# Another order table for the first two thirds of an attention and mixture-of-experts kernel

## The chip, the cores and the metric

The kernel runs on one core of one Trainium2 chip. The metric is the device time of one execution in microseconds (us). The kernel before took 322.93 us, the median of three runs (321.3 to 323.65).

## The reference, cut to what matters

Three computations follow one another, all in float32.

1. **Linear attention** (2 batches, 8 heads, 576 tokens, head size 64, 128 features): `phi(x) = exp(h - max h)` with `h = x·omegaᵀ` less a row constant; then `kv = Σ k_p vᵀ`, `z = Σ k_p`, and `out = (q_p·kv) / (q_p·z + 1e-6)`.
2. **A gated product**: `a = x@w1`, `b = x@w2`, `h = (a*b)@w3`, `out = h@w_out`, with 1152 tokens, 512 model columns and 1024 inner columns. The two last products have nothing between them, so the kernel forms `W = w3@w_out` once.
3. **Mixture of experts**: `logits = x@w_gate`, `argmax` over 8 experts, softmax weight of the winner; every token goes to its expert (`w1`, relu, `w2`) as far as capacity lasts and is scaled by its weight.

The weights of part 2 come as 64-bit words; the kernel turns them into float32 on the chip.

## The kernel before, in words

A table, `ORDER` (line 36), is a list of words. Each word is one step (`t_` and the letters), its arguments, and behind `@` the bank of the matmul results that it takes. A loop runs the words from first to last, and what each step issues then stands in that order on its engine: on TensorE (PE), VectorE (DVE), ScalarE (ACT), GpSimd (POOL) and the DMA queue of SyncE (SP). Each of them works its own list strictly in order. A second string, `END`, orders what comes behind the table: the rest of part 2, the routing and the experts; it stays.

The steps that the prediction speaks of, with their lines:

- `LD`, `LDV`, `LDOM`, `LDCAP` (L241, L246, L231, L491): loads by SP: one of nine blocks of 128 tokens of k or q (256 KB), of v (260 KB), omega, and the capacity, which is spread to 96 partitions. `ZD` and `ZG` store zeros.
- `PJ.k1` (L253): the projection of a block on PE into a pair of banks. `MX` (L258): its row maxima on DVE. Then either `E0` and `E1` (L274): eight exponentials on ACT straight out of the banks, or `SUB` (L266) on DVE, which frees the banks, and `EX` (L269) on ACT. The next `PJ` of a pair waits until its banks are free.
- `KO` (L227) opens a pair of banks for the sums over tokens, `KV` (L299) adds a block of k to them, `KVZ` (L306) reads them out.
- `TR` (L310) transposes q on PE, `NUM` (L325) forms the numerators, `RD`, `X`, `XT`, `XH`, `XL` divide, transpose and split x in a high and a low part.
- A weight tile goes through `LDW` (L374, 512 KB, two raw buffers), `WA`, `WB`, `WC` (L381, L384, L387: three bit operations on DVE), `CAST` (L392, ACT, the high part) and `LOW` (L396, POOL, the low part, in one subtraction). The next but one `LDW` waits for this tile's `WC`. There are 40 tiles, `w10` to `w27`, `wo0` to `wo7` and `w300` to `w371`.
- `AB` (L403) is twelve matmuls of a tile with x; `ASB` and `G` (L408, L413) read and multiply; `TT` (L533) and `ST` (L538) turn the product and store it in DRAM. `W` (L427) forms the combined weight, `WR`, `WH`, `WL` read it out. `GT`, `GU`, `UC`, `LG` carry the gate through it.

Of the kernel before, what the change touches and what calls it, by code (L numbers as in the profile page):

```python
# [40 lines left out]
PJ.q2@2 EX.k8 WB.w12 KO.1@0 KV.6 MX.q2 EX.q1 KV.4b WC.w12 E0.q2 KV.7 MX.q4 LDW.w10 LD.q8 KV.5 E1.q2 WB.w20 KV.8 WC.w20 CAST.w12 MX.q3 LDW.w11 TR.2.0@2
KVZ.1 LOW.w12 TR.0.0@3 QT.2.0 TR.0.1@0 SUB.q3 TR.2.1@1 QT.0.0 TR.1.1@2 QT.0.1 WA.w10 TR.1.0@3 QT.2.1 WB.w10 NUM.0@6 QT.1.0 WC.w10 NUM.2@0 QT.1.1 RD.0
LDW.w13 E0.q4 X.0 NUM.1@2 RD.2 X.2 XT.0@6 CAST.w20 RD.1 XT.2@7 XH.0 LOW.w20 X.1 TR.4.0@0 XH.2 XL.0 XT.1@1 PJ.q6@2 XL.2 XH.1 CAST.w10 XL.1 PJ.q5@6
E1.q4 LOW.w10 MX.q6 AB.2.0.0@1 WA.w11 EX.q3 WB.w11 AB.0.0.0@4 E1.q6 WC.w11 MX.q5 LDW.w21 AB.0.0.1@5 CAST.w11 SUB.q5 QT.4.0 LOW.w11 ASB.0.0 TR.4.1@0
ASB.2.0 G.0.0 TR.3.0@4 WA.w13 TR.3.1@1 QT.3.0 AB.1.0.0@5 WA.w21 QT.3.1 WB.w13 QT.4.1 WB.w21 E0.q6 NUM.3@6 WC.w21 NUM.4@0 WC.w13 LDW.w22 CAST.w21 RD.3
LDW.wo0 PJ.q8@2 ASB.1.0 LOW.w21 RD.4 EX.q5 X.3 PJ.q7@4 X.4 CAST.w13 MX.q8 XT.3@6 LOW.w13 XT.4@7 XH.3 AB.1.0.1@0 XH.4 XL.3 E0.q8 XL.4 AB.3.0.0@1 MX.q7
E1.q8 AB.0.1.0@6 WA.w22 WB.w22 WC.w22 TR.5.1@7 ASB.0.1 AB.0.1.1@2 WA.wo0 LDW.w23 CAST.w22 WB.wo0 SUB.q7 LOW.w22 AB.1.1.0@3 WC.wo0 TR.6.1@6 G.0.1
CAST.wo0 LDW.w14 AB.2.1.0@4 TT.0.0 ASB.1.1 LOW.wo0 G.1.0 AB.2.0.1@5 WA.w23 WB.w23 WC.w23 AB.2.1.1@0 WA.w14 LDW.w300 WB.w14 AB.1.1.1@2 WC.w14 G.2.0
CAST.w14 LDW.wo2 AB.3.1.0@3 CAST.w23 G.1.1 TT.1.0 ASB.2.1 LOW.w23 EX.q7 TR.6.0@2 G.2.1 TR.5.0@5 LOW.w14 QT.6.0 TT.2.0 TR.7.0@4 QT.5.0 TR.8.0@0
AB.3.0.1@2 QT.5.1 WA.wo2 QT.6.1 WA.w300 WB.w300 ASB.3.0 NUM.6@6 QT.8.0 WB.wo2 NUM.5@0 QT.7.0 WC.wo2 ASB.3.1 WC.w300 LDW.wo3 CAST.wo2 AB.3.1.1@3 RD.6  # L50
LDW.w24 CAST.w300 RD.5 X.6 LOW.w300 TR.7.1@5 X.5 XT.6@4 QT.7.1 TR.8.1@6 G.3.0 LOW.wo2 AB.4.1.0@7 G.3.1 QT.8.1 TT.3.0 XH.6 XT.5@5 WA.wo3 ST.0.0.1
NUM.7@0 XL.6 ST.0.0.3 XH.5 XL.5 NUM.8@2 WB.wo3 AB.3.2.0@6 WA.w24 WB.w24 WC.wo3 AB.0.2.0@4 WC.w24 CAST.wo3 LDW.w320 ASB.3.2 RD.8 LOW.wo3 LDW.wo1
AB.1.2.0@5 CAST.w24 X.8 ST.0.0.2 RD.7 X.7 LOW.w24 AB.2.2.0@6 WA.w320 AB.0.2.1@2 WB.w320 ASB.2.2 WC.w320 XT.8@3 WA.wo1 CAST.w320 LDW.wo6 XT.7@6
ST.0.0.0 WB.wo1 XH.8 AB.3.2.1@0 XH.7 LOW.w320 XL.8 ASB.1.2 XL.7 AB.2.2.1@1 WC.wo1 CAST.wo1 LDW.w310 WA.wo6 AB.0.3.0@3 G.3.2 LOW.wo1 ASB.0.2 G.0.2
WB.wo6 AB.1.3.0@6 WC.wo6 WA.w310 CAST.wo6 LDW.wo4 AB.0.3.1@0 WB.w310 ASB.0.3 WC.w310 AB.2.3.0@5 G.0.3 CAST.w310 LOW.wo6 LDW.wo7 TT.0.1 ASB.1.3
AB.4.3.0@4 LOW.w310 CONSTV LGM@0 WA.wo4 AB.1.2.1@6 WB.wo4 WA.wo7 AB.1.3.1@2 WC.wo4 WB.wo7 CAST.wo4 LDW.wo5 AB.2.3.1@3 WC.wo7 G.1.3 LOW.wo4 LDW.w301
G.1.2 ASB.2.3 AB.3.3.0@2 G.2.2 CAST.wo7 TT.1.1 ASB.4.3 LOW.wo7 W.0.0@6 G.2.3 ASB.3.3 TT.2.1 ASB.4.1 WA.w301 WB.w301 AB.3.3.1@1 WA.wo5 WC.w301
AB.4.1.1@7 CAST.w301 LDW.w350 G.3.3 TT.3.1 LOW.w301 W.1.0@1 ST.0.1.0 WB.wo5 WC.wo5 WA.w350 CAST.wo5 LDW.w351 ST.0.1.3 WB.w350 AB.4.0.0@5 WC.w350
CAST.w350 LOW.wo5 LDW.w15 AB.4.3.1@4 ST.0.1.1 LOW.w350 W.0.1@-1 WA.w351 WB.w351 WC.w351 W.5.0@3 LDW.w321 CAST.w351 WA.w15 G.4.1 WH.0 LOW.w351 WR.0
WB.w15 W.2.0@2 WC.w15 CAST.w15 LDW.w360 WA.w321 WB.w321 WC.w321 AB.4.2.0@7 LOW.w15 LDW.w16 ST.0.1.2 AB.4.2.1@6 WA.w360 ASB.4.2 CAST.w321 WB.w360  # L60
WC.w360 W.5.1@-1 G.4.2 CAST.w360 LOW.w321 LDW.w370 WA.w16 WB.w16 AB.5.1.0@7 WH.5 WC.w16 CAST.w16 LOW.w360 LDW.w311 AB.5.0.0@6 ASB.5.1 ASB.4.0 WA.w370
G.4.3 LOW.w16 W.2.1@-1 WB.w370 WC.w370 AB.6.0.0@7 WA.w311 CAST.w370 LDW.w340 WB.w311 WR.2 WC.w311 AB.4.0.1@5 CAST.w311 LOW.w370 LDW.w330 WH.2 W.6.0@4
LOW.w311 G.4.0 WA.w340 WB.w340 W.1.1@-1 WC.w340 WA.w330 CAST.w340 LDW.w341 TT.4.1 LOW.w340 GT.0@2 WB.w330 WR.1 AB.6.1.0@5 ASB.6.0 WC.w330 WR.5 WA.w341
LDW.w331 WH.1 W.4.0@7 WB.w341 CAST.w330 WC.w341 TT.4.0 LOW.w330 LDW.w361 W.7.0@3 CAST.w341 WA.w331 LOW.w341 WA.w361 W.4.1@-1 WB.w331 WC.w331 WB.w361
CAST.w331 LDW.w371 WC.w361 W.3.0@1 CAST.w361 LOW.w331 LDW.w25 ASB.5.0 LOW.w361 W.3.1@-1 WA.w371 WB.w371 WC.w371 WA.w25 CAST.w371 LDW.w26 GT.1@6 WB.w25
WTC.0 W.6.1@-1 WTC.1 WC.w25 WH.3 LOW.w371 LDW.w17 CAST.w25 WR.3 LOW.w25 W.7.1@-1 WH.4 WA.w26 WB.w26 WC.w26 WG@2 AB.5.0.1@6 WGC WA.w17 LDW.w27 WR.6
WB.w17 CAST.w26 WC.w17 GU.0@1 GU.1@2 UC.0 LOW.w26 LG.0 UC.1 CAST.w17 LG.1 G.5.0 ASB.6.1 WL.2 AB.5.1.1@1 WR.4 WR.7 LOW.w17 AB.6.1.1@2 G.5.1 TT.5.0 WL.1
GT.2@5 G.6.1 GT.5@1 WA.w27 AB.7.1.0@6 WTC.5 WB.w27 WC.w27 AB.7.0.0@7 CAST.w27 LOW.w27 AB.6.0.1@2 ASB.7.0 WL.5 AB.7.0.1@1 G.6.0 WL.4 TT.6.0 GT.6@7 WH.6
# [1033 lines left out]
```

## Time and profile before

| What | Value |
|---|---|
| median of three runs | 322.93 us |
| the profiled execution's own time | 322.64 us |
| its span | 320.9 us |
| PE busy | 307.9 us (96%) |
| DVE / ACT / POOL busy | 209.3 / 130.4 / 107.4 us |
| granted TensorE clock, mean | 0.999 |

The span is the profiled stretch of the execution; 1.74 us of the execution's own time lie around it. An engine's busy time is the union of its instructions; what is left of the span it waited. A row of a timeline gives the start, the length, the engine, the line and operation, how many instructions are merged, and in brackets the idle time before and what ended it.

### The profile page before, as it was taken

The page shows a single profiled execution, that of the slowest core. Times are in us where ns is not written, and L with a number is a line of the kernel's source. Part 1 is how long each engine was busy: PE and PEld are TensorE (multiplying, and loading weights), DVE is VectorE, ACT ScalarE, POOL GpSimd, SP SyncE. Part 2 cuts the span into 40 slices and gives each one's busy share as a digit, 9 for nine tenths or more (in the row PEclk, how much of TensorE's full clock was granted, in tenths as well). Part 3 has the DMA queues.
Part 4 walks back from the last instruction along what each step waited for, and adds up shares of the span by engine and source line. Part 5 has one row for each costly group of instructions (what it writes and reads, how often), then busy time and mean ns, then how long its engine had stood idle before and what let it go on. Part 6 is the DMA issues. An engine that isn't in the chain of part 4 may idle for free. (4 is left out here: it accounts for less than half of the span.)

```text
span 320.9 us, 7411 instructions
## 1 busy us (share of the span) xinstructions
PE 307.9 (96%) x3045; PEld 286.9 (89%) x3045; DVE 209.3 (65%) x381; ACT 130.4 (41%) x301; POOL 107.4 (33%) x96
## 2 busy tenths in 40 slices
...
GB/s 180 401 314 385 193 68 77 122 137 127 176 183 185 133 132 163 211 171 160 167 131 151 178 2 2 141 11 251 161 237 150 203 231 66 93 133 49 1 27 53
DMA packets 25180, 47.77 MB, mean 149 GB/s; under 512 B 3148, under 2 KB 12492, under 8 KB 25142
## 3 DMA queue, kind: packets, MB, share of 16 engines
...
q10 hardware_dynamic: 2368, 1.18, 2.8%
...
q14 instruction: 13, 0.11, 0.1%
...
## 5 line engine op out<-in xcount | busy, mean ns | idle before, releaser
L403 PE MATMUL banks<-xh,w_hl 128*128 128x288 f32 x416 | 87.9, 298 | 1.1 <-DVE g L413 1.0
L396 POOL TENSOR_TENSOR w_hl<-w_f,w_hl 128x512 fp32r<-128x512 f32 x32 | 43.6, 1364 | 111.1 <-ACT w_hl L392 111.1
L403 PEld LDWEIGHTS banks<-xh,w_hl 128*128 128x128 f32 x416 | 67.9, 188 | 2.4 <-DVE g L413 1.2
L403 PE MATMUL banks<-xl,w_hl 128*128 128x288 f32 x208 | 61.4, 295 | 0.0
L427 PE MATMUL banks<-wo_hl,w_hl 128*128 128x512 f32 x192 | 46.0, 395 | 0.0
L427 PEld LDWEIGHTS banks<-wo_hl,w_hl 128*128 128x128 f32 x192 | 35.5, 188 | 7.9 <-POOL w_hl L396 0.2
L392 ACT CAST w_hl<-w_f 128x512 fp32r<-128x512 f32 x32 | 20.0, 627 | 49.5 <-DVE w_f L387 49.4
L403 PEld LDWEIGHTS banks<-xl,w_hl 128*128 128x128 f32 x208 | 39.1, 188 | 0.2
L387 DVE SCALAR_TENSOR_TENSOR w_f<-w_raw,w_f 128x512 uint32<-128x512 uint32 x32 | 28.8, 903 | 0.9
L381 DVE TENSOR_SCALAR w_f<-w_raw 128x512 uint32<-128x512 uint32 x32 | 17.8, 555 | 16.3 <-DMA w_raw<-in_w 13.7
L258 DVE TENSOR_REDUCE mx<-banks 128x8 f32<-128x1024 f32 x18 | 21.6, 1218 | 9.5 <-PE banks L253 9.1
L814 PE MATMUL banks<-r_xc,W 128*128 128x288 f32 x192 | 26.8, 297 | 0.0
L814 PEld LDWEIGHTS banks<-r_xc,W 128*128 128x128 f32 x192 | 25.8, 188 | 0.1
L384 DVE SCALAR_TENSOR_TENSOR w_f<-w_raw,w_f 128x512 uint32<-128x512 uint32 x32 | 24.6, 772 | 0.8
L533 DVE STREAM_TRANSPOSE gs<-g 128x576 f32<-128x576 f32 x16 | 19.8, 1238 | 4.4 <-POOL g L562 4.1
L553 PE MATMUL banks<-xh,w_hl 128*128 128x288 f32 x96 | 20.2, 299 | 0.0
L396 POOL TENSOR_TENSOR wo_hl<-wo_f,wo_hl 128x512 fp32r<-128x512 f32 x8 | 11.4, 1431 | 18.8 <-ACT wo_hl L392 18.8
L413 DVE TENSOR_TENSOR g<-a_sb,banks 128x288 f32<-128x288 f32 x26 | 11.5, 448 | 9.0 <-PE banks L403 5.6
L731 POOL TENSOR_TENSOR r_e_00l<-r_e_0r,r_e_00h 128x512 fp32r<-128x512 f32 x4 | 6.0, 1512 | 30.4 <-ACT r_e_00h L727 15.1
L553 PEld LDWEIGHTS banks<-xh,w_hl 128*128 128x128 f32 x96 | 15.7, 188 | 0.6 <-issue 0.5
L408 ACT COPY a_sb<-banks 128x288 f32<-128x288 f32 x26 | 10.2, 403 | 12.7 <-PE banks L403 9.4
L852 POOL DMA_INDIRECT out<-r_yo,r_odx x6 | 5.6, 938 | 25.6 <-DVE r_yo L849 16.4
...
## 6 DMA issues: line engine op xcount, KB each, us to landing
w_raw<-in_w SPq DMA_DIRECT2D x32, 512.0 KB, 4.5
wo_raw<-in_wo SPq DMA_DIRECT2D x8, 512.0 KB, 4.6
...
r_e_0r<-in_e SPq DMA_DIRECT2D x4, 512.0 KB, 4.1
```

The source lines that it names most:

```text
L258: V.tensor_reduce(out=mx, in_=heads(at["pj", n]), axis=AX, op=ALU.max, negate=True)
L381: V.tensor_scalar(out=f, in0=word(w, 1), scalar1=3, scalar2=0x3FFFFFF8, op0=ALU.logical_shift_left, op1=ALU.bitwise_and)
L384: V.scalar_tensor_tensor(out=words_of[w], in0=word(w, 1), scalar=0xC0000000, in1=words_of[w], op0=ALU.bitwise_and, op1=ALU.bitwise_or)
L387: V.scalar_tensor_tensor(out=words_of[w], in0=word(w, 0), scalar=29, in1=words_of[w], op0=ALU.logical_shift_right, op1=ALU.bitwise_or)
L392: A.copy(out=t[:, 0], in_=words_of[w].bitcast(F32))
L396: nc.gpsimd.tensor_tensor(out=h[1], in0=words_of[w].bitcast(F32), in1=h[0].bitcast(F32), op=ALU.subtract)
L403: nc.tensor.matmul(out=banks[:, b, :C], lhsT=hl[s][:, k, :], rhs=xhl[int(c)][r][:, k], start=(n == 0), stop=(n == 11))
L413: V.tensor_tensor(out=g_t[int(f)][:, int(c) * C:(int(c) + 1) * C], in0=abp.pop((f, c)), in1=banks[:, at["ab", f, c, "1"], :C], op=ALU.mult)
L427: nc.tensor.matmul(out=banks[:, at["W", f]], lhsT=w[s][:, k % 4, :], rhs=hl_of[f"wo{k}"][r], start=(k == 0 and (s, r) == (0, 0)), stop=(k ...
L533: V.transpose(out=sts[f // GF, b][:, :, :, f % GF], in_=g_t[f][:, b * S:(b + 1) * S].rearrange("p (j t) -> p j t", t=32))
L553: nc.tensor.matmul(out=p[:, :C], lhsT=hl[s][:, k, :], rhs=xhl[c][r][:, k], start=(n == 0), stop=(n == 11))
L814: nc.tensor.matmul(out=p4[d][:, :C], lhsT=w_t[f][:, s, d * 128:(d + 1) * 128], rhs=xc[r][f // 4][:, f % 4], start=(f == 0 and (s, r) == (0 ...
```

## The change

The 31 lines of `ORDER` are replaced by 31 others: the same kinds of steps on the same data in another order, many with other banks. The table was found by a search that scores a table as the mean over several draws of durations. Nothing else is changed: no step's code, not `END`, no buffer count. Two lines of the table, of 62 in the difference:

```diff
 ORDER = """
-LD.k1 CONST WU@0 LDOM LD.k3 LDCAP LD.k4 LDW.w20 LD.q0 LD.k2 OMS IDENT LD.k6 LD.k0 PJ.k1@2 LD.k5 ZM LDV.3 ZG.1 PJ.k4@4 MX.k1 PJ.k3@6 MX.k4 E0.k1 LDV.1
...
+LDOM CONST WU@0 LD.k1 LD.q0 LD.k4 LD.k0 LD.k6 LD.k3 OMS LDV.4 ZM LD.k2 IDENT LD.k5 PJ.k1@2 LDV.2 PJ.q0@4 MX.k1 LDV.1 PJ.k4@6 LD.k7 MX.q0 E0.k1 PJ.k0@0
...
```

**TensorE, the first projections.** `k1_97` is the block k1, `om_s` the scaled omega; each row is eight matmuls, one `PJ`. Before:

```order
L253 MATMUL banks_84<-om_s_87,k1_97 128x128 x8
L253 MATMUL banks_84<-om_s_87,k4_134 128x128 x8
L253 MATMUL banks_84<-om_s_87,k3_131 128x128 x8
L253 MATMUL banks_84<-om_s_87,q0_138 128x128 x8
L253 MATMUL banks_84<-om_s_87,k0_149 128x128 x8
L253 MATMUL banks_84<-om_s_87,k5_159 128x128 x8
L253 MATMUL banks_84<-om_s_87,k2_140 128x128 x8
```

Now:

```order
L253 MATMUL banks_84<-om_s_87,k1_129 128x128 x8
L253 MATMUL banks_84<-om_s_87,q0_131 128x128 x8
L253 MATMUL banks_84<-om_s_87,k4_133 128x128 x8
L253 MATMUL banks_84<-om_s_87,k0_135 128x128 x8
L253 MATMUL banks_84<-om_s_87,k3_139 128x128 x8
L253 MATMUL banks_84<-om_s_87,k5_152 128x128 x8
L253 MATMUL banks_84<-om_s_87,k2_146 128x128 x8
```

The first four projections take the four pairs of banks; q0 and k0 moved in front of k3, which is now the first that reuses a pair (k1's). On DVE the maxima of k1, q0, k4 and k0 now stand in a row, and `SUB.k4`, `MX.k3`, `SUB.k0`, `MX.k5`, `MX.k2`, `SUB.k2` follow; before it was the maxima of k1, k4, k3, then `SUB.k4`, the maxima of q0 and k0, and `SUB.k0`.

**The DMA queue of SP.** Its head before:

```order
L241 DMA k1_97<-in_kT 128x512
L231 DMA om_sb_129<-in_om 128x256
L241 DMA k3_131<-in_kT 128x512
L491 DMA cap_u_89<-in_cap 96x2
L241 DMA k4_134<-in_kT 128x512
L374 DMA w20_raw_136<-in_w2 128x1024
L241 DMA q0_138<-in_qT 128x512
```

Where the capacity's load stands now, with the stores of zeros (`out_0`) around it:

```order
L241 DMA q5_371<-in_qT 128x512
L241 DMA q6_425<-in_qT 128x512
L374 DMA w10_raw_545<-in_w1 128x1024
L477 DMA out_0<-zero_144 128x3x512
L491 DMA cap_u_89<-in_cap 96x2
L374 DMA w13_raw_591<-in_w1 128x1024
L374 DMA w11_raw_671<-in_w1 128x1024
```

The capacity went from fourth to 37th place, behind the load of w10; the first weight tile also left the head (it is now 19th), and one store of zeros stands between w10 and w13. Before, all stores of `out` stood in front of w10.

**VectorE, the weight tiles in the middle.** `w310_f` is the tile that `WA`, `WB` and `WC` make. Before:

```order
L381 TENSOR_SCALAR wo1_f_1450<-wo1_raw_1390 128x512
L384 SCALAR_TENSOR_TENSOR wo1_f_1450<-wo1_raw_1390,wo1_f_1450 128x512
L362 TENSOR_TENSOR xl3_1303<-banks_84,xh3_1302 128x4x128 x2
L387 SCALAR_TENSOR_TENSOR wo1_f_1450<-wo1_raw_1390,wo1_f_1450 128x512
L381 TENSOR_SCALAR wo6_f_1498<-wo6_raw_1454 128x512
L413 TENSOR_TENSOR g3_1283<-a_sb_1383,banks_84 128x288
L413 TENSOR_TENSOR g0_831<-a_sb_1514,banks_84 128x288
L384 SCALAR_TENSOR_TENSOR wo6_f_1498<-wo6_raw_1454,wo6_f_1498 128x512
L387 SCALAR_TENSOR_TENSOR wo6_f_1498<-wo6_raw_1454,wo6_f_1498 128x512
```

Now:

```order
L381 TENSOR_SCALAR wo1_f_1469<-wo1_raw_1407 128x512
L384 SCALAR_TENSOR_TENSOR wo1_f_1469<-wo1_raw_1407,wo1_f_1469 128x512
L387 SCALAR_TENSOR_TENSOR wo1_f_1469<-wo1_raw_1407,wo1_f_1469 128x512
L381 TENSOR_SCALAR w310_f_1489<-w310_raw_1446 128x512
L384 SCALAR_TENSOR_TENSOR w310_f_1489<-w310_raw_1446,w310_f_1489 128x512
L387 SCALAR_TENSOR_TENSOR w310_f_1489<-w310_raw_1446,w310_f_1489 128x512
L413 TENSOR_TENSOR g0_1042<-a_sb_1422,banks_84 128x288
L362 TENSOR_TENSOR xl3_1290<-banks_84,xh3_1289 128x4x128
L413 TENSOR_TENSOR g3_1268<-a_sb_1530,banks_84 128x288
L381 TENSOR_SCALAR wo6_f_1547<-wo6_raw_1491 128x512
L384 SCALAR_TENSOR_TENSOR wo6_f_1547<-wo6_raw_1491,wo6_f_1547 128x512
L387 SCALAR_TENSOR_TENSOR wo6_f_1547<-wo6_raw_1491,wo6_f_1547 128x512
```

The three operations of a tile now mostly stand together; other work went between tiles. Over the last 26 tiles (w320 on), eleven tiles had something between their `WA` and `WC` before, and five have it now.

## Rows read from the trace of the kernel before

**Rows 1.** The page: busy us of each engine (share of the span), instructions.
```profile
PE 307.9 (96%) x3045; PEld 286.9 (89%) x3045; DVE 209.3 (65%) x381; ACT 130.4 (41%) x301; POOL 107.4 (33%) x96
```

**Rows 2.** PE's waits: total us, times, longest.
```profile
PE banks L253 <- DMA k<-in_kT: 3.3, 3, 1.3
...
PE banks L403 <- DVE g L413: 1.0, 1, 1.0
```

**Rows 3.** PE by stretch: length, busy us (instructions), clock, DMA share, GB/s.
```profile
5.13:36.66 31.53, 26.06 (x550) 1.00 0.94 338
36.66:113.70 77.04, 76.93 (x846) 1.00 0.48 132
113.70:116.00 2.30, 1.33 (x10) 1.00 0.64 198
116.00:203.07 87.07, 86.83 (x771) 1.00 0.48 135
203.07:315.90 112.83, 112.73 (x861) 1.00 0.48 123
```

**Rows 4.** PE's timeline at the start.
```profile
5.13 1.51 PE L253 MATMUL banks<-om_s,k 64*128 64x128 f32 x16
7.71 2.06 PE L253 MATMUL banks<-om_s,k 64*128 64x128 f32 x32 [1.07 <-DMA k<-in_kT]
...
15.98 0.38 PE L227 MATMUL banks<-zeros 128*128 128x260 f16 x2 [1.22 <-DVE k0p L266]
16.29 1.15 PE L299 MATMUL banks<-v,k3p 128*64 128x65 f32 x32
...
36.66 0.66 PE L310 MATMUL banks<-ident,q2p 128*128 128x128 f32 x4
```

**Rows 5.** DVE's timeline at the start.
```profile
6.69 1.22 DVE L258 TENSOR_REDUCE mx<-banks 128x8 f32<-128x1024 f32 x1 [6.69 <-PE banks L253]
8.92 2.36 DVE L258 TENSOR_REDUCE mx<-banks 128x8 f32<-128x1024 f32 x2 [1.01 <-PE banks L253]
...
18.23 1.22 DVE L266 TENSOR_TENSOR k2p<-banks,mx 128x1024 f32<-128x1024 f32 x1
19.37 1.21 DVE L258 TENSOR_REDUCE mx<-banks 128x8 f32<-128x1024 f32 x1
```

**Rows 6.** ACT's timeline at the start.
```profile
7.95 2.17 ACT L274 ACTIVATE k1p<-banks,mx 128x128 f32<-128x128 f32 x8 [3.62 <-DVE mx L258]
...
19.11 1.11 ACT L269 ACTIVATE k0p<-k0p 128x1024 f32<-128x1024 f32 x1
```

**Rows 7.** DMA in 0 to 3.9 us, in 3.9 to 6.4, in 6.4 to 14.4.
```profile
DMA packets 359, 0.53 MB, mean 136 GB/s; under 512 B 37, under 2 KB 165, under 8 KB 359
...
DMA packets 270, 0.30 MB, mean 121 GB/s; under 512 B 126, under 2 KB 126, under 8 KB 270
...
DMA packets 1453, 3.17 MB, mean 397 GB/s; under 512 B 161, under 2 KB 161, under 8 KB 1453
```

**Rows 8.** DVE's waits, the longest line.
```profile
DVE w_f L381 <- DMA w_raw<-in_w: 13.7, 14, 3.1
```

**Rows 9.** Waits of PE's weight loads.
```profile
PEld banks L427 <- POOL w_hl L396: 0.2, 1, 0.2
```

**Rows 10.** DVE by line, 20 to 36 us: busy us, mean ns, idle before.
```profile
L387 DVE SCALAR_TENSOR_TENSOR w_f<-w_raw,w_f 128x512 uint32<-128x512 uint32 x2 | 1.4, 688 | 0.0
...
L381 DVE TENSOR_SCALAR w_f<-w_raw 128x512 uint32<-128x512 uint32 x2 | 0.8, 418 | 0.0
```

**Rows 11.** DVE by line, 100 to 190 us.
```profile
L387 DVE SCALAR_TENSOR_TENSOR w_f<-w_raw,w_f 128x512 uint32<-128x512 uint32 x20 | 20.6, 1031 | 0.7
L384 DVE SCALAR_TENSOR_TENSOR w_f<-w_raw,w_f 128x512 uint32<-128x512 uint32 x20 | 16.4, 820 | 0.5
L381 DVE TENSOR_SCALAR w_f<-w_raw 128x512 uint32<-128x512 uint32 x20 | 12.7, 633 | 13.1 <-DMA w_raw<-in_w 10.6 <-POOL w_hl L396 2.4
```

**Rows 12.** DMA issues: KB each, median us to landing.
```profile
w_raw<-in_w SPq DMA_DIRECT2D x32, 512.0 KB, 4.5
```

More of the change, by code (lines that the diff above doesn't have):

```diff
@@ L41 @@
[L41 to L68, printed above, removed]
@@ L69 @@
-WL.3 G.7.0 GT.3@2 WTC.2 AB.7.1.1@4 WTC.3 WTC.6 GU.3@1 GU.5@5 UC.3 GU.2@2 ASB.7.1 LG.3 UC.2 G.7.1 UC.5 GT.7@1 TT.7.0 GT.4@2 WTC.7 LG.2 WTC.4 ST.1.0.1
-GU.6@1 LG.5 ST.1.0.2 UC.6 ST.1.0.3 GU.4@2 GU.7@1 ST.1.0.0 UC.4 LG.6 UC.7 WH.7 LG.4 WL.7 WL.0 WL.6
+LDOM CONST WU@0 LD.k1 LD.q0 LD.k4 LD.k0 LD.k6 LD.k3 OMS LDV.4 ZM LD.k2 IDENT LD.k5 PJ.k1@2 LDV.2 PJ.q0@4 MX.k1 LDV.1 PJ.k4@6 LD.k7 MX.q0 E0.k1 PJ.k0@0
+LD.q8 LDV.0 MX.k4 E1.k1 LDV.3 MX.k0 LD.q1 E1.q0 LD.k8 PJ.k3@2 SUB.k4 LDW.w20 ZG.1 E0.q0 MX.k3 PJ.k5@6 LDWG LDV.5 SUB.k0 E1.k3 PJ.k2@4 LDV.6 LDW.w12
```

35 lines of the change are left out of this document (32 added, 3 removed).

## The prediction, on record before the changed kernel ran

> **What bounds the kernel now.** I read the page first: PE is busy for 96% of the span, every other engine for 65% or less [rows 1]. So I asked when PE is not busy, stretch by stretch [rows 3]. The reader should see how uneven it is. From 5.13 to 36.66 us, where PE runs the projections and the sums over k, it idles 31.53 - 26.06 = 5.47 us. From there to its last matmul it idles 0.11 + 0.97 + 0.24 + 0.10 = 1.42 us in 279 us, and 0.97 of that is one gap near 115 us, where an `AB` waited for the `G` that frees its bank [rows 2, 3]. The granted clock is 1.00 in every stretch, so nothing is to be had there. The change keeps all matmuls; it can win or lose only idle time of PE: some 6.9 us at most, 5.5 of it at the start.
>
> The start is paced by two things. One is the loads: three gaps, 3.3 us, end with a block of k landing [rows 2]. The other is DVE: it begins at 6.69 us, waits 1.01 us for the second projection, and PE then waits 1.22 us for `SUB.k0` [rows 4, 5]. The DMA rows tell why k4 was late: from 3.9 to 6.4 us the queue moved 121 GB/s with 126 packets under 512 B, behind that 397 GB/s [rows 7]. The capacity's load (96 rows of one word, fourth in the queue) stands there. At the later rate the 2.5 us would have moved 0.99 MB and not 0.30: a loss of 1.7 us for all loads behind it.
>
> **The start, step by step.** Durations are those of before: a projection 1.03 us (two in 2.06), the first one 1.51; a `KV` about 1.1 [rows 4]; `MX` and `SUB` 1.22 us long and 1.14 from start to start (18.23 to 19.37) [rows 5]; eight exponentials 2.17 us, an `EX` 1.1 [rows 6].
>
> PE starts k1 at 5.13 us as before (the warm-up matmuls set that), then q0, k4 and k0 without a pause, until about 9.75 us. Their loads and omega are 1.18 MB (four times 0.262 and 0.131). Even if the slow 2.5 us came all the same, 0.53 + 0.30 MB would have moved by 6.4 us, and k0 would be in 0.9 us later at 397 GB/s, at about 7.3 us, before PE wants it at 8.7 [rows 7]: the gain does not hang on my reading of the capacity.
>
> DVE, from 6.69 us in steps of 1.14: `MX` k1, q0 7.83, k4 8.97, k0 10.11, `SUB.k4` 11.25, `MX.k3` 12.39, `SUB.k0` 13.53, `MX.k5` 14.67, `MX.k2` 15.81, `SUB.k2` 16.95, and so on to `SUB.q1` 22.65 and `SUB.k8` 25.8, with the first steps of two weights (0.42 us each) in between [rows 5, 10].
>
> PE then waits three times. k3 takes k1's banks and waits for its exponentials, 7.95 + 2.17 = 10.1 us [rows 6]: 0.35 us. k5 waits for `SUB.k4`, 11.25 + 1.22 = 12.47, having been free at 11.2: 1.3 us. `KO.0` waits for `SUB.k0`, 14.75, having been free at 14.55: 0.2 us. After that PE has `KV`s between its projections and, step by step, comes at about the moment it may: k7 needs `SUB.k2` (18.2) and PE is there at 18.2; q2 needs `SUB.q1` (23.9) and PE is there at 24.5; `KO.1` needs `SUB.k8` (27.0) and PE is there at 27.6. That makes 1.85 us of idle time; with 0.15 for the tight ones, 2.0 against 5.47. **First term: -3.5 us**, and the first transposes come at about 33.2 us rather than 36.66 [rows 4]. Bounds: -3.6 (no other wait) and -2.5 (each of the three tight places 0.3 us late).
>
> The other engines come along. DVE's own list up to the same point (all maxima, `SUB.q3`, the first two weights) ends near 34.0 us, as against 37.6, so it is ahead by as much. The first `LDW` that waits for a raw buffer goes out behind `WC.w12` at about 29.3 us, not 32.6.
>
> **The rest of the table.** Here no sum can be made of removed work, since nothing is removed. Before, waits after 36.66 us come to 1.42 us. The gap of 0.97 has its cause in one place of the old order (a `G` that stood in DVE's list behind the operations of two tiles, wo4 and wo7), and that sequence is gone; but an order unknown to the trace will have small waits of its own. Their bounds are 0 and, from a weight path that does not follow (first rival), about 3 us; nearest are the 1.42 us that the old order had here. I take 0.8. **Second term: 0.8 - 1.42 = -0.6 us.**
>
> Edits that I cost at nothing: other banks (what waits is in the walk above); the stores of zeros and the capacity moved behind w10 (the capacity is first used in the middle of the table; the cover of these transfers is the time until w11 is due, third rival); the stores of the products, twelve as before; the `END` part, whose instructions are the same and whose 112.83 us hold 0.10 us of idle time [rows 3]: it begins earlier by what the table gains. If that cover went, a late store would show as PE waiting for the gathered rows.
>
> **Sum.** The profiled execution's own time is 322.64 us, 1.74 us above its span, and 0.3 below the median of the runs. 322.64 - 3.5 - 0.6 = **318.5 us**.
>
> **Rivals.** First: **the weights give it back.** Between 100 and 190 us a tile is made only just in time. DVE waited 14 times, 13.7 us, for a raw tile [rows 8], since two buffers and 4.5 us from issue to landing [rows 12] leave it dry; PE's weight load once waited 0.2 us for a `LOW` [rows 9], so there is no reserve in places. PE comes 3.5 us earlier; if the path gains only its earlier beginning less 0.1 us on each of the last 26 tiles, 2.6 us go back: 321.1 us, and all between 319.8 and 322.2. For it: those rows. Against it: the new order breaks up five of these tiles between `WA` and `WC` where the old one broke up eleven, and each break holds back a raw buffer, so the path should get shorter. Chance 0.22.
>
> Second: **DVE and POOL block each other more.** `WC` took 688 ns while POOL was idle [rows 10] and 1031 ns on average later, `WB` 820, `WA` 633 rather than 418 [rows 11]; POOL's subtractions are what is new there. A tile costs DVE about 0.7 us more than alone. Six tiles more now run unbroken, so that a `LOW` falls on the next tile's `WA` and `WB` and not on other work; at 0.7 us for each, 4.2 us of DVE time come on the weights' path, and the whole gain is gone: 322.6 us. It needs every one of them to reach PE, and DVE's 13.7 us of waiting for loads would swallow them first. Chance 0.07. The Trainium skill (SBUF — State Buffer, "Who interferes with whom") has this as a rule: a DVE instruction with two SBUF inputs contends with a GpSimd instruction that reads SBUF, and the one that comes second is fully blocked. By that rule, `WB` and `WC` can lose a whole `LOW` each time and packing them is no help; `WA`, with one input, would only lose where it runs in a two-port mode, and the rows show that it does lose.
>
> Third, on the other side: **the capacity's load blocks the weights.** It now stands behind w10 and a store of zeros, and in front of w13 and w11. If its small packets hold the queue not for 2.5 us but for far longer, w13 and w11 land late, DVE stops at `WA.w11` with the maxima of q6 and q5 behind it, and PE runs dry. By the walk, the queue is through w10 and the store (1.3 MB from 29.7 us at 397 GB/s) at 33.0 us; then the capacity, then two tiles in 2.6 us; DVE wants w11 at about 42.4 us. So it costs nothing up to 6.8 us, and each further microsecond is one of the whole. Before it took 2.5 us. At 15 us, six times that, the stop is 8.2 us: 326.7 us. Chance 0.03.
>
> That the change does nothing at the start would need PE's waits to stand in the loads alone; but the loads of the first four blocks are early by 2 us or more (above).
>
> **Numbers.** The forecast has 0.65 and its own range is 317.3 (no new wait, 322.64 - 3.6 - 1.42, and 0.3 for the spread of runs) to 319.7. With the first rival nearly whole, the range is 317.3 to 322.2; what is left out is the second rival, the slower side and still larger gains. A difference of 1% is 3.2 us, about what a measurement tells from none; against 322.93 that limit is 319.7. Faster by more: 0.66 (the forecast and a little); within: 0.29 (the first two rivals); slower: 0.05 (the third, and a like one that I have not seen).
>
> **What would show it.** In the new profile: PE's idle time between 5.13 us and its first transpose near 2.0 us, with waits by exponentials of k1, by `SUB.k4` and `SUB.k0` and none of a microsecond by a load; the first transpose at 33 to 33.5 us; DVE without the gap of 1.01 us; few packets under 512 B before 10 us and some between 30 and 36; DVE's wait for raw tiles below 13.7 us; no PE gap of over 0.5 us behind. Wrong would be: the first transpose later than 34.2 us (the walk failed); or that it is early and gaps by `LOW`, `G` or `w_hl` add up to more than 2 us between 100 and 200 us (first rival); or `WC` above 1031 ns with no change in time (second).

## The result, and the profile after

The changed kernel takes 317.83 us (median of six runs, 316.6 to 320.73) where the kernel before took 323.27 on the same chip (six runs, 321.3 to 324.94): a ratio of 0.9863, 95% interval 0.9824 to 0.9902. The profiled execution took 317.38 us with a span of 315.6, 5.3 less than before. The forecast was 318.5, as a ratio 318.5 / 322.93 = 0.986. The quotient of the two medians is 0.983; every ratio here and below is the measured one that comes with an interval.

The page of the changed kernel, and PE's waits (total us, times, longest), in answer to [rows 1] and [rows 2]:

```profile
PE 306.6 (97%) x3045; PEld 286.8 (91%) x3045; DVE 210.9 (67%) x381; ACT 131.2 (42%) x301; POOL 106.0 (34%) x96
...
PE banks L253 <- DVE k4p L266: 1.2, 1, 1.2
...
PE banks L253 <- ACT k1p L274: 0.5, 1, 0.5
...
PE banks L227 <- DVE k0p L266: 0.2, 1, 0.2
```

In this execution no block of k is waited for. What is left of the start's waits are the three that the walk named. PE by stretch (length, busy us, clock, DMA share, GB/s), in answer to [rows 3]: from the first projection to the first transpose, from there to `END`, and `END`:

```profile
4.81:32.29 27.48, 25.62 (x549) 1.00 0.90 321
32.29:197.12 164.83, 164.57 (x1625) 1.00 0.50 145
197.12:309.95 112.83, 112.74 (x861) 1.00 0.48 124
```

Idle time at the start fell from 5.47 to 1.86 us, and between there and `END` from 1.32 to 0.26. `END` takes 112.83 us in both. PE's timeline at the start, against [rows 4]:

```profile
4.81 1.16 PE L253 MATMUL banks<-om_s,k 64*128 64x128 f32 x16
5.80 1.06 PE L253 MATMUL banks<-om_s,q 64*128 64x128 f32 x16
...
9.50 1.16 PE L253 MATMUL banks<-om_s,k 64*128 64x128 f32 x14 [0.50 <-ACT k1p L274]
11.82 2.06 PE L253 MATMUL banks<-om_s,k 64*128 64x128 f32 x32 [1.16 <-DVE k4p L266]
14.08 0.38 PE L227 MATMUL banks<-zeros 128*128 128x260 f16 x2 [0.20 <-DVE k0p L266]
...
32.29 0.66 PE L310 MATMUL banks<-ident,q0p 128*128 128x128 f32 x4
```

The first transpose comes 4.37 us earlier than in [rows 4], 0.9 more than forecast, although the waits come to what was forecast. The first line says where most of the 0.9 is: k1 began 0.32 us before the walk's 5.13 and lasted 1.16 us and not 1.51, so that DVE began at 6.02 and not at 6.69. Against [rows 5], DVE has lost its gap of 1.01 us:

```profile
6.02 4.62 DVE L258 TENSOR_REDUCE mx<-banks 128x8 f32<-128x1024 f32 x4 [6.02 <-PE banks L253]
10.55 1.22 DVE L266 TENSOR_TENSOR k4p<-banks,mx 128x1024 f32<-128x1024 f32 x1
```

DMA from 3.9 to 6.4 us, against [rows 7], and from 30 to 36 us, where the capacity's load now runs:

```profile
DMA packets 481, 0.87 MB, mean 350 GB/s; under 512 B 54, under 2 KB 54, under 8 KB 481
...
DMA packets 780, 1.78 MB, mean 297 GB/s; under 512 B 159, under 2 KB 159, under 8 KB 778
```

The 100 or so small packets moved from the one stretch to the other (30 to 36 us had 56 of them before), and PE waits nowhere for the weights behind them. DVE's wait for raw tiles, the raw tiles' loads (KB, median us to landing) and the three steps of a tile between 100 and 190 us (mean ns), against [rows 8], [rows 12] and [rows 11]:

```profile
DVE w_f L381 <- DMA w_raw<-in_w: 14.2, 13, 2.7
```

```profile
w_raw<-in_w SPq DMA_DIRECT2D x32, 512.0 KB, 4.0
```

```profile
L387 DVE SCALAR_TENSOR_TENSOR w_f<-w_raw,w_f 128x512 uint32<-128x512 uint32 x19 | 19.2, 1009 | 0.6
L384 DVE SCALAR_TENSOR_TENSOR w_f<-w_raw,w_f 128x512 uint32<-128x512 uint32 x19 | 17.8, 935 | 0.6
L381 DVE TENSOR_SCALAR w_f<-w_raw 128x512 uint32<-128x512 uint32 x19 | 9.9, 524 | 12.2 <-DMA w_raw<-in_w 12.0
```

The weights' path does not look shorter here: the wait is 14.2 us where it was 13.7, though a load lands in 4.0 us and not in 4.5, and the three steps of a tile take 524 + 935 + 1009 = 2468 ns where they took 2484. But one trace each does not settle it. In a second execution of the changed kernel (e5 below) the same wait is

```profile
DVE w_f L381 <- DMA w_raw<-in_w: 18.1, 15, 2.9
```

and over all traces below it is 12.9 to 18.1 us with the new order of the tiles (nine traces) and 13.7 to 18.6 with the old (five).

### The profile page after: what moved, and what is told of

Its sections match the earlier page's. It is cut to its first block, busy times and chain, and to the rows that moved or that the text cites. A ratio compares the mean times of both kernels' runs of the same rounds, so it can differ in the third digit from the quotient of the medians.

```text
span 315.6 us, 7420 instructions
## 1 busy us (share of the span) xinstructions
PE 306.6 (97%) x3045; PEld 286.8 (91%) x3045; DVE 210.9 (67%) x381; ACT 131.2 (42%) x301; POOL 106.0 (34%) x96
## 4 chain that ended last, share of the span: by engine, by line
PE 95%; DVE 3%; POOL 0%; issue 0%; POOLq 0%; ACT 0%
PE banks L403 27%; PE banks L427 14%; PE banks L814 8%; PE banks L836 8%; PE banks L553 6%; PE banks L876 5%; PE banks L919 4%; PE banks L253 4%; PE banks L299 3%; PE banks L325 3%; PE banks L310 3%; DVE mx L258 2%; PE banks L797 2%; PE banks L573 2%; PE banks L343 1%; PE banks L288 1%
## 5 line engine op out<-in xcount | busy, mean ns | idle before, releaser
L396 POOL TENSOR_TENSOR w_hl<-w_f,w_hl 128x512 fp32r<-128x512 f32 x32 | 42.5, 1333 | 107.5 <-ACT w_hl L392 106.1
L387 DVE SCALAR_TENSOR_TENSOR w_f<-w_raw,w_f 128x512 uint32<-128x512 uint32 x32 | 28.1, 878 | 0.9
L384 DVE SCALAR_TENSOR_TENSOR w_f<-w_raw,w_f 128x512 uint32<-128x512 uint32 x32 | 27.7, 865 | 0.8
L381 DVE TENSOR_SCALAR w_f<-w_raw 128x512 uint32<-128x512 uint32 x32 | 15.8, 492 | 14.4 <-DMA w_raw<-in_w 14.2
L841 DVE SCALAR_TENSOR_TENSOR r_h<-banks,r_h 128x288 fp32r<-128x288 f32 x16 | 7.1, 455 | 10.6 <-ACT r_h L840 9.5
```

The source lines that it names most:

```text
L381: V.tensor_scalar(out=f, in0=word(w, 1), scalar1=3, scalar2=0x3FFFFFF8, op0=ALU.logical_shift_left, op1=ALU.bitwise_and)
L384: V.scalar_tensor_tensor(out=words_of[w], in0=word(w, 1), scalar=0xC0000000, in1=words_of[w], op0=ALU.bitwise_and, op1=ALU.bitwise_or)
L387: V.scalar_tensor_tensor(out=words_of[w], in0=word(w, 0), scalar=29, in1=words_of[w], op0=ALU.logical_shift_right, op1=ALU.bitwise_or)
L396: nc.gpsimd.tensor_tensor(out=h[1], in0=words_of[w].bitcast(F32), in1=h[0].bitcast(F32), op=ALU.subtract)
```

## The experiments

All kernels in one view. In the diffs below dots stand for words left out. The idle time is PE's, in us; at the start it counts from PE's first projection, so a wait for k1 itself (0.80 us in e5, 1.14 in e11) stands ahead of it; "rest" runs from the first transpose to PE's last matmul; the last column is what the span has behind that matmul. All but the ratio come from one traced execution of each kernel.

| kernel | ratio to before, 95% | idle at the start | first transpose | rest (idle in it) | behind PE |
|---|---|---|---|---|---|
| before | 1 | 5.47 | 36.66 | 279.2 (1.4) | 5.0 |
| changed | 0.9863, 0.9824 to 0.9902 | 1.86 | 32.29 | 277.7 (0.35) | 5.7 |
| e5, changed again | 0.9859, 0.9825 to 0.9892 | 1.92 | 33.52 | 278.3 (0.4) | 8.4 |
| e1, capacity first | 0.9882, 0.9842 to 0.9922 | 1.92 | 33.44 | 279.9 (1.35) | 5.5 |
| e12, new table, old loads | 0.9896, 0.9844 to 0.9949 | 3.36 | 33.86 | 278.3 (0.6) | 5.5 |
| e2, old table, capacity late | 0.9954, 0.9918 to 0.9989 | 5.30 | 35.60 | 279.1 (0.9) | 5.1 |
| e9, old table, weights late | 0.9917, 0.9878 to 0.9955 | 2.49 | 33.18 | 280.6 (1.5) | 5.2 |
| e3, new start, old rest | 0.9922, 0.9890 to 0.9954 | 1.92 | 32.28 | 280.6 (1.9) | 7.3 |
| e6, the same, banks changed | 0.9935, 0.9906 to 0.9964 | 1.71 | 34.01 | 280.0 (1.3) | 7.3 |
| e4, old start, new rest | 0.9994, 0.9957 to 1.0031 | 5.50 | 37.10 | 278.2 (0.6) | 5.4 |
| e7, start reordered | 0.9891, 0.9847 to 0.9935 | 1.87 | 32.70 | 278.5 (0.8) | 6.3 |
| e8, short warm-up | 0.9841, 0.9810 to 0.9872 | 2.10 | 32.41 | 279.7 (1.7) | 5.5 |
| e10, start by DVE | 0.9815, 0.9763 to 0.9868 | 1.11 | 32.80 | 278.5 (0.8) | 5.9 |
| e11, e10 and short warm-up | 0.9799, 0.9748 to 0.9850 | 1.65 | 33.04 | 278.6 (0.9) | 5.6 |

**e1: the capacity at the head of the new table's queue.**

```diff
-LDOM CONST WU@0 LD.k1 LD.q0 LD.k4 LD.k0 LD.k6 LD.k3
-... LDW.w10 ZD.1 LDCAP E1.q2
+LDOM CONST WU@0 LD.k1 LD.q0 LDCAP LD.k4 LD.k0 LD.k6 LD.k3
+... LDW.w10 ZD.1 E1.q2
```

> The new table with one word moved: the capacity's load stands fifth in the queue again, right behind q0, and not behind w10. Theory ORDER (the gain at the start comes from which blocks are projected first): PE wants k0 only at 7.6 us, so the loads of k4 and k0, even 1.7 us later, are just in time; first transpose at 32.3 to 32.6 us (changed kernel 32.29, before 36.66), time 317.4 to 318.1. Rival LOAD (the gain comes from taking the capacity's load off the head of the queue): 121 GB/s for 2.5 us comes back, waits of PE for k blocks of 1.7 us or more, first transpose at 34.0 or later, time 319.1 or more.

PE's timeline of e1, and its DMA from 3.9 to 6.4 us:

```profile
5.13 1.99 PE L253 MATMUL banks<-om_s,k 64*128 64x128 f32 x16
6.96 1.06 PE L253 MATMUL banks<-om_s,q 64*128 64x128 f32 x16
...
33.44 0.66 PE L310 MATMUL banks<-ident,q0p 128*128 128x128 f32 x4
```

```profile
DMA packets 552, 0.80 MB, mean 322 GB/s; under 512 B 160, under 2 KB 160, under 8 KB 552
```

The first transpose is 1.15 us late, outside what ORDER allowed, but no load is waited for: the same three waits come to the same 1.9 us. The delay is all there when the second projection begins (6.96 and not 5.80): the first one began 0.32 us later and took 0.83 us more. With the small packets back in the stretch the queue still moved 0.80 MB, 0.07 less than without. So LOAD's mechanism fell, for this order of blocks. The time did not come as ORDER had it: 320.56 us (before 323.66) lies where LOAD forecast it, with 1.35 us of idle time in the rest and a ratio whose interval holds the changed kernel's 0.986; the times do not decide.

**e2: the capacity late in the old table.**

```diff
-LD.k1 CONST WU@0 LDOM LD.k3 LDCAP LD.k4 LDW.w20
-... LDW.w10 LD.q8
+LD.k1 CONST WU@0 LDOM LD.k3 LD.k4 LDW.w20
+... LDW.w10 LDCAP LD.q8
```

> The table of before with one word moved: the capacity's load goes behind w10's, as in the changed kernel. Theory ORDER: the two waits for k4 and k0 (1.07 and 0.96 us) shrink, but DVE still works the blocks in the old order and PE still waits for SUB.k0, then for a late block; first transpose between 35.3 and 36.2 us, so at most 1.4 of the 4.4 us, time 321.3 to 322.3. Rival LOAD: first transpose at 33.5 or earlier, 3 us or more of the 4.4; time 319.6 or less.

As ORDER said in place and time: 1.06 us at the first transpose, 322.07 us (12 runs). Not so in the waits, which stay:

```profile
PE banks L253 <- DMA k<-in_kT: 3.2, 3, 1.4
```

They stay because PE came earlier too: k1 began at 4.51 and not at 5.13 us and was at full speed, and k4 was projected at 6.49 and not at 7.71. Is that 1.2 us the capacity's price? DMA from 3.9 to 6.4 us in e2, then in e4 (below), whose queue begins as before, and PE's start in e4:

```profile
DMA packets 362, 0.87 MB, mean 349 GB/s; under 512 B 32, under 2 KB 32, under 8 KB 362
...
DMA packets 348, 0.50 MB, mean 200 GB/s; under 512 B 142, under 2 KB 142, under 8 KB 348
...
5.13 3.82 PE L253 MATMUL banks<-om_s,k 64*128 64x128 f32 x48
```

With the capacity at the head the old queue moved 0.30 and 0.50 MB, without it 0.87; but in e4 PE does not wait for k4 at all. So the price is open in the old order, and 1.7 us is more than any pair of traces shows.

**e3 and e6: the new start with the old rest.**

```diff
 LDOM CONST WU@0 LD.k1 LD.q0 LD.k4 LD.k0
 ...
-SUB.q3 LDW.w13 TR.0.0@6 KVZ.1 LOW.w12
+SUB.q3 LDW.w11 ZG.0 ZD.0 MX.q4
+(the words of the table before that are left, in its order; e6 with banks 0, 1 and 2, 3 exchanged)
```

> The new table up to its first transpose (w11 in the place of w13 in the queue), and from there the steps that are left in the order of before. Theory ORDER with an unchanged second part: first transpose at 32.3, PE's idle time behind it as before (about 1.4 us, the 0.97 us wait of an AB for G at 110 us among it), time 322.6 - 4.4 = 318.2, 317.8 to 318.8. Rival WEIGHTS (the old order of the weight tiles has no reserve and gives the gain back when PE comes earlier): PE's idle time behind the first transpose at 3.5 us or more, with waits by LOW, G or w_hl, time 320.3 to 321.5.

> As e3, with banks 0 and 1 exchanged for 2 and 3 in the old rest, so that no step overwrites the sums of the second batch. Theory ORDER with an unchanged second part: PE's idle time behind the first transpose 1.0 to 1.9 us, its end 280 to 281 us behind the first transpose, time 318 to 320 and a ratio to before of 0.985 to 0.990. Rival WEIGHTS: 3.5 us or more of idle time there, ratio 0.995 or more.

In e3 a transpose overwrites part of the second batch's sums over k before they are read out, so it computes other data with the same instructions; e6 leaves them alone. Both gain 2.1 to 2.5 us, where the changed kernel gains 4.4 to 4.6. Their idle time in the rest is 1.9 and 1.3 us (0.7 of e3's is at that transpose), less than the 3.5 that WEIGHTS asked for. But ORDER's times fell too: e3's 321.45 us lie where WEIGHTS forecast them, and e6's ratio of 0.9935 lies between the two. The rest as a whole takes 280.6 and 280.0 us, 1 us more than with the old, late start, and 1.6 us more than in the changed kernel follow PE's last matmul. I can't place all of that. Another part of e6's time is not the table's: its granted clock was 0.95 in the first 33 us, and the first transpose came at 34.01 for it. The fall lies between 12 and 16 us, where PE had just waited 0.55 and 1.16 us:

```profile
0.00:33.00 33.00, 30.17 (x536) 0.95 0.83 289
...
12.00:14.00 2.00, 1.77 (x16) 0.54 1.07 405
14.00:16.00 2.00, 2.00 (x22) 0.61 1.03 395
```

**e4: the old start with the new rest.**

```diff
 LD.k1 CONST WU@0 LDOM LD.k3 LDCAP LD.k4 LDW.w20
 ...
-LDW.w11 TR.2.0@2 KVZ.1 LOW.w12
+LDW.w13 SUB.q3 TR.0.0@6 KVZ.1 LOW.w12
+(the words of the new table that are left, in its order)
```

> The table of before up to its first transpose (w13 in the place of w11 in the queue), and from there the steps that are left in the new order. Both terms as measured add up: first transpose at 36.7 us, idle time of PE behind it 0.4 us where it was 1.4, time 321.0 to 321.8. If instead the new order of the rest is needed only because PE comes early, or pays nothing: idle time 1.2 us or more, time 322.3 to 323.

The trace agrees with the first: 0.56 us of idle time in the rest, which is 1.1 us shorter than before's. The time, 323.15 us, does not show it and lies above both ranges: at the joint the first transpose waits 0.69 us for `SUB.q3`, because in this mix it takes a bank that the projection of q3 still holds. The two halves do not add up: -2.1 for the new start alone, nothing for the new rest alone, -4.5 for both, each with about 1.2 us of uncertainty.

**e5: the changed kernel once more.**

> The changed kernel itself once more. In six traces so far PE's matmuls took twice their later time at first (warm-up 215 to 218 ns from start to start, then 111) and the step to the short ones came anywhere from 3.8 to 7 us. Theory STEP (that moment belongs to the execution, not to the kernel, and the new table feels all of it): PE's three waits at the start come to 1.8 to 2.0 us again, and the first transpose stands at 32.29 us plus what the warm-up and the first projections take longer than in the first trace, so anywhere from 31.9 to 33.6; ratio to before 0.983 to 0.992. Rival LOAD (the first trace of the changed kernel and the one with the capacity at the head differ by the capacity): the step at the same moment as in the first trace, first transpose at 32.2 to 32.4.

319.71 us, before 323.93 in the same session. PE's timeline, and POOL's waits at the end of the span:

```profile
5.88 1.16 PE L253 MATMUL banks<-om_s,k 64*128 64x128 f32 x16 [0.80 <-DMA k<-in_kT]
...
33.52 0.66 PE L310 MATMUL banks<-ident,q0p 128*128 128x128 f32 x4
```

```profile
POOL out L852 <- DVE r_yo L849: 10.4, 1, 10.4
POOL out L852 <- DMA out<-r_yo,r_odx: 4.8, 1, 4.8
POOL out L852 <- issue: 4.5, 1, 4.5
```

STEP was right on the waits and the place of the first transpose, but it was a second accident that put it there: PE was at speed early, and waited 0.80 us for k1, whose load, issued at 1.21 us as in the first trace, landed 4.5 us later and not 2.5. This profiled execution took 321.95 us, the slowest of its six, and the page says why: 1.2 us at the start, and 2.8 us more than the first trace behind PE's last matmul, where POOL held the last scatter back for 4.5 us. The third line (a wait for nothing that the profile shows) is absent in the first trace; e3 and e6 have it too (7.3 us behind PE). What released it late is not shown; in these three the scatters landed a median 4.5 to 4.8 us after their issue, in the first trace 3.4.

**e8: 12 warm-up matmuls.**

```diff
-        for k in range(18):
+        for k in range(12):
...
```

> The changed kernel with 12 warm-up matmuls and not 18 (they end near 3.74 us; k1 landed at 3.76, omega was scaled at 3.42). Theory STEP: PE is busy all the same, only with projections, so the moment of the step does not change; k1 begins at 3.8 us and DVE's first maxima 0.1 to 1.1 us earlier, and so does the first transpose; time 0.1 to 1.0 us less. Rival WARM (the step needs the warm-up's matmuls, or comes later for projections): the first three projections at the long time, first transpose 0.5 us or more later than for 18, time the same or more.

```profile
1.12 2.78 PE L288 MATMUL banks<-zeros 128*128 128x260 f16 x12 [1.12 <-POOL zeros L200]
4.04 1.68 PE L253 MATMUL banks<-om_s,k 64*128 64x128 f32 x16
```

The projections do bring the step: k1 began at 4.04, was slow in its first part, and the second projection began at 5.54, sooner than in any other trace. PE then waits 0.29 us for k4. First transpose at 32.41, between the changed kernel's 32.29 and 33.52, so WARM fell; that the short warm-up gains, as STEP has it, is not shown: 0.7 us less than e5 on the same chip lies inside both intervals.

**e7: reorder the start by PE's longest wait.**

```diff
-MX.k4 E1.k1 LDV.3 MX.k0 ... SUB.k4 ... MX.k3 PJ.k5@6 LDWG LDV.5 SUB.k0
+MX.k4 E1.k1 LDV.3 SUB.k4 MX.k0 ... SUB.k0 MX.k3 PJ.k5@6 EX.k4 EX.k0 KO.0@4 KV.1 E1.k3 PJ.k2@0
...
-PJ.k2@4 ... KO.0@0 ... KV.1 ... PJ.k6@2 ... KV.3
+... KV.4a KV.0 PJ.k6@2 ... KV.3
(behind these, banks 0 and 1 exchanged with 4 and 5)
```

> The changed kernel with twelve words of its start moved: SUB.k4 ahead of MX.k0 and SUB.k0 ahead of MX.k3 on DVE, EX.k4 and EX.k0 ahead of k3's exponentials on ACT, and on PE the order k5, KO.0, KV.1, k2, KV.4a, KV.0, k6 (KO.0 takes q0's banks, k2 takes k0's, and so on with 0, 1 and 4, 5 exchanged). By the walk with the trace's durations k5's wait of 1.16 us and KO.0's of 0.20 go; 0.5 for k3 stays, and about 0.5 comes at q4 or q2 near 23 us: idle time at the start 1.0 us and not 1.86, first transpose 0.5 to 0.9 us earlier for the same step of PE's speed, time 0.2 to 1.0 us less. Rival DVE (DVE works without a pause from 6 us on and sets the pace, so a wait only changes its place): idle time at the start still 1.7 to 2.2 us, time the same.

My walk failed and the rival DVE was right: idle time 1.87 us, time 320.28. The wait for `SUB.k4` is down to 0.16 us, and as much stands elsewhere (PE, then DVE):

```profile
24.35 2.95 PE L253 MATMUL banks<-om_s,q 64*128 64x128 f32 x48 [1.13 <-DVE q1p L266]
```

```profile
23.07 1.23 DVE L266 TENSOR_TENSOR q1p<-banks,mx 128x1024 f32<-128x1024 f32 x1
```

DVE had paused for 0.23 us since its first maximum. PE can't be ahead of an engine that never rests, however its own list is turned; what counts is which of DVE's operations stand ahead of the one that PE needs.

**e9: the old table with its loads alone moved.**

```diff
-LD.k1 CONST WU@0 LDOM LD.k3 LDCAP LD.k4 LDW.w20 LD.q0 ... LDW.w12 ... LD.k8 ... LD.k7 ... LDV.5 ... LDW.w10
+LD.k1 CONST WU@0 LDOM LD.k3 LD.k4 LD.q0 ... LD.k8 ... LD.k7 LDW.w20 ... LDV.5 LDW.w12 ... LDW.w10 LDCAP
```

> The table of before with three words moved, loads alone: the capacity behind w10 as in e2, w20 (512 KB) from ahead of q0 and k0 to behind k7, and w12 from ahead of k8 and k7 to behind the fifth block of v. No load of a weight then stands ahead of a block of k. Theory ORDER (the old order of blocks leaves DVE's SUB.k0 where it was, so waits by loads turn into waits by DVE): waits of PE for k blocks 0.9 us or less in place of 3.2, its wait for SUB.k0 at 1.5 us or more, first transpose at 34.6 to 35.6 us (e2 35.60, before 36.66, changed kernel 32.29 to 33.52); time 321 to 322.3. Rival LOADS (the gain of the new table is its order of loads): idle time at the start 2.5 us or less, first transpose at 33.8 or earlier, ratio to before 0.990 or less.

```profile
PE banks L227 <- DVE k0p L266: 1.3, 1, 1.3
...
PE banks L253 <- DVE k4p L266: 0.5, 1, 0.5
...
PE banks L253 <- DMA k<-in_kT: 0.4, 1, 0.4
```

Here my theory fell. I had expected the waits by loads to turn into waits by DVE; 2.8 of the 3.2 us went, and the waits by DVE came to 2.1 us where they had been 1.0 in e2. Three loads out of the way bring the old table's first transpose to 33.18. The largest of the waits, 1.4 us for k7 behind two weights, left only 0.3 us for DVE in its place. The time, 321.02 us, fell short of LOADS, because in its trace the rest took 1.4 us more than before.

**e12: the new table with the old loads.**

```diff
-LD.q0 LD.k4 LD.k0 ... LDV.1 ... LDW.w20 ... LDW.w12 ... LDW.w10 ZD.1 LDCAP
+LD.q0 LDCAP LD.k4 LDW.w20 LD.k0 ... LDV.1 LDW.w12 ... LDW.w10 ZD.1
```

> The other half of e9: the changed kernel with the three loads where the table before had them (the capacity fourth in the queue, w20's 512 KB sixth, right behind k4 and ahead of k0, w12's behind the second block of v); the order on PE, DVE and ACT is the new one. Theory LOADS (after e9: the start's gain lies in which loads stand ahead of the blocks of k): before, w20 was in at 8.98 us behind the same amount of data, so k0 comes at about 9.6, k3 at 11.0 and k5 at 13 us, where PE wants them at 7.6 to 8.6, 10 and 12; PE waits 1.5 to 3 us for loads, first transpose 1.5 to 2.5 us later than the changed kernel's for the same step of PE's speed (33.8 to 36 us), time 320 to 322, ratio 0.990 to 0.996. Theory ORDER (the new order of blocks alone gives the gain): waits for loads under 0.5 us, first transpose as in the changed kernel's traces (32.3 to 33.6), ratio 0.988 or less.

```profile
PE banks L253 <- DMA k<-in_kT: 1.4, 3, 0.9
...
PE banks L299 <- DMA v<-in_v: 0.7, 1, 0.7
```

2.1 us of waits by loads, and yet a first transpose at 33.86, at the early end of LOADS, with a ratio in between. So neither theory holds alone. The loads are worth 3 us at idle time in the old order (5.47 to 2.49) and 1.5 in the new one (3.36 to 1.86); the order of blocks 2.1 us with the old loads and 0.6 with the new. Either removes most of the same waits. These sums are rough: the end of k1's projection, which is not the table's, differs by up to 0.9 us between these traces, and moves the waits for loads. By the first transpose the loads alone bring 3.5 us (36.66 to 33.18), the order alone 2.8, both together 3.1 to 4.4, which says the same.

**e10 and e11: a start ordered by DVE's list.** The diff is against e7.

```diff
-SUB.k6 PJ.q1@6 ... MX.k7 EX.k2 MX.q1 E1.k7 PJ.k8@2 SUB.q1 ... WA.w20 MX.k8 ... WA.w12 EX.q1 SUB.k8
+SUB.k6 MX.q1 EX.k2 SUB.q1 ... MX.k8 SUB.k8 PJ.q2@6 KVZ.0 PJ.q3@4 EX.q1 MX.k7 EX.k8 E1.k7 KO.1@2 KV.5 WA.w20 WA.w12
```

> The start of e7, reordered further by what its trace shows: DVE never pauses, and KO.1 goes out when SUB.k8 ends, so the first transpose follows SUB.k8 by 5.4 us. On DVE MX.q1, SUB.q1, MX.k8 and SUB.k8 go ahead of MX.k7, and both WA behind it; on PE q1 goes ahead of k7, and q3 and KO.1 ahead of q4; the exponentials of k7 come later. Theory DVE: SUB.k8 ends at about 25.3 us where e7 had 27.2, PE's wait for q2 (1.13 us) goes, idle time at the start 0.6 to 1.0 us, first transpose 31.4 to 32.0 for e7's step of PE's speed (up to 0.5 more or less for another); time 0.5 to 1.5 us below the changed kernel's (ratio 0.980 to 0.985). Rival: k7's later exponentials hold q4 or KV.7 and ACT becomes the pace: idle time 1.7 us or more, no gain over the changed kernel.

> As e10, and 12 warm-up matmuls and not 18 as in e8. Theory DVE: DVE's first maxima 0 to 1.1 us earlier than in e10, PE then waits for loads of k4 or k0 by some tenths as in e8 (0.14 and 0.29 us); first transpose at 31.0 to 31.8, ratio to before 0.977 to 0.984. Rival: the loads take all of it, first transpose and time as in e10.

PE in e10, and the DVE operation that it follows:

```profile
26.14 0.38 PE L227 MATMUL banks<-zeros 128*128 128x260 f16 x2 [0.40 <-DVE k8p L266]
```

```profile
24.86 1.23 DVE L266 TENSOR_TENSOR k8p<-banks,mx 128x1024 f32<-128x1024 f32 x1
```

Idle time at the start is 1.11 us, just over the 1.0 that was forecast. `SUB.k8` ends at 26.1, not 25.3, and the first transpose at 32.80 missed its range, as e11's 33.04 did; in this trace the second projection began at 6.77 us, 0.78 later than in e7, which is most of both. 318.09 us for e10 and 317.68 for e11, before 323.87: the two best ratios of all. Whether they beat the changed kernel by more than the measurement's error is not settled, since the intervals overlap (0.9815 and 0.9799 against 0.986). In e11 the execution that was traced had k1 landing late again and PE waiting 1.14 us for it, so what the short warm-up gives is not seen there; against e10 it is within the error.

## Why the prediction came out right, point by point

**The waits at the start: right.** Forecast 0.35 for k3, 1.3 for k5, 0.2 for `KO.0` and 0.15 for tight places; measured 0.50, 1.16, 0.20 and none. The first term, -3.5 us of idle time, is 5.47 - 1.86 = 3.6, and 5.50 with the old start in e4 against 1.92 with the new one in e3 and e5. By its own terms the lower bound would be 5.47 - 1.85 - 0.9 = 2.7 and not 2.5. The walk builds the new start up from its own steps, so it did not need to know that 0.9 of the old 5.47 us end with nothing that the profile shows (PE's waits before):

```profile
PE banks L299 <- issue: 0.9, 2, 0.6
```

That the loads of the first four blocks are early by 2 us or more was misread: the walk itself has k0 at 7.3 us for 8.7, and PE waited 0.80 us for k1 in e5 and 1.14 in e11.

**The first projection: a number that is none of the table's.** The walk took 5.13 and 1.51 us from [rows 4]. In the traces it starts between 4.04 and 5.88 us and lasts 1.16 to 1.99. The old start hid that: PE then waited for a load anyway [rows 2]. The new one does not, and passes it on whole. From DVE's first maximum to the first transpose it is 26.27, 26.27 and 26.44 us in the changed kernel, e1 and e5 (DVE begins at 6.02, 7.17 and 7.08); the walk has 33.2 - 6.69 = 26.5. So of the 0.9 us by which the first transpose beat the forecast, 6.69 - 6.02 = 0.67 are luck of that execution, 0.15 are the tight places that cost nothing, and e5 with 33.52 has the other luck.

**"The gain does not hang on my reading of the capacity": right.** e1 shows it: no wait for a load with the capacity at the head. The reading itself, a price of 1.7 us, no run bears out (e1 none, e4 no wait for k4, e2 at most 1.2). But the prediction spoke of the capacity and not of w20 and w12, which were the larger part of what stood ahead of the blocks (e2: 1.06 us at the first transpose; e9: 2.4 more). The sum held because the walk had all loads of the new table in it.

**The second term, -0.6: right in sign, too small in the first trace.** Idle time behind the first transpose went from 1.4 to 0.35 us, and to 0.4 in e5; I had 0.8. The stretch as a whole is 1.6 and 1.0 us shorter. (In the first trace the span's 5.3 us are 4.4 of first transpose and 1.6 of this stretch, less 0.65 behind PE.) In other kernels with this rest it has 0.6 to 1.7 us of idle time, so 0.8 was not a bad mean of what an execution has. The gap of 0.97 us at 115 us is gone, and the cause named for it holds: between 100 and 116 us PE waits 0.4 to 1.0 us for a `G` or an `ASB` in all five traces with the old rest and in none of the nine with the new, four of which have a smaller wait for a `G` (0.3 to 0.7) later. What the sum took for granted, that the two terms add, the times do not show: -2.1, nothing and -4.5 us (e6, e4, e5).

**First rival, the weights give it back: not in the new rest; in the old, open.** In no trace of the new rest does PE wait more than 0.2 us for a `LOW`, or its weight loads more than 0.6. With the early start the old rest took 280.0 to 280.6 us (e3, e6, e9) and 279.1 to 279.2 with the late one (before, e2); but single traces of the new rest lie between 277.7 and 279.9. My sign, DVE's wait below 13.7 us, did not come (14.2, and 18.1 in e5), and could not have told the orders apart: it differs by 4 us between two executions of one kernel. Why the new rest keeps the gain is therefore open.

**Second rival, DVE against POOL: no.** In the first trace `WB` went up by 115 ns and `WA` down by 109, but in e5 `WB` took 788. The three steps of a tile together take 2289 to 2468 ns in the nine traces with the new rest and 2445 to 2555 in the five with the old, so the packed tiles cost no more. That a DVE instruction with two SBUF inputs, as `WB` is one, contends with a GpSimd instruction that reads SBUF is what the Trainium skill says (SBUF — State Buffer, "Who interferes with whom"); the traces agree as far as they go, 820 and 935 ns between 100 and 190 us against 688 and 683 between 20 and 36, where POOL had next to no subtractions, but no run here takes POOL away. **Third, the capacity in front of w13: no**; 297 GB/s there, and no wait of PE.

**The end of the span** was left out of the sum, as unchanged. It is unchanged in its instructions, but had 5.0, 5.7 and 8.4 us behind PE's last matmul. That error is as large as any term of the second half.
